# A retention and two feed-forward stages on one core: the order of the opening, and how weight conversions mix with the other vector work

## The chip, the cores and the metric

The kernel runs on one core of a Trainium2 chip. The metric is device time in microseconds (us), taken as the median of several runs of the whole kernel; a separate, profiled execution gives the trace. The engines are TensorE (PE in the rows; its weight loads are PEld), VectorE (DVE), ScalarE (ACT), GpSimd (POOL) and SyncE (SP), whose work here is to issue DMAs.

## What is computed

There are 2 sequences of 768 positions with 8 heads of 64. The retention works block by block with a state per head; `lam` is a decay rate per head:

```python
intra = einsum('bhic,bhjc->bhij', qb, kb) * Dmask       # lam ** (i - j), i >= j
out   = einsum('bhij,bhjd->bhid', intra, vb) + einsum('bhid,bhde->bhie', qb * lam_pow, kv_state)
kv_state = lam_block * kv_state + einsum('bhsd,bhse->bhde', kb * rev_pow, vb)
```

Its output, as 1536 tokens of 512, goes through two feed-forward stages: `relu(x @ w_in) ** 2 @ w_out` with 2048 inner columns, and `(sigmoid(x @ w_gate) * (x @ w_val)) @ w_out` with 1536. All inputs and the output are 32-bit floats.

## The kernel before, in words

Every matmul of the feed-forward stages is done in three passes (high part of the weights by high part of the data, low by high, high by low), so each operand is split: ScalarE copies the high part (`whi`, `gh`, `xh`), VectorE subtracts it from the source to get the low part (`wlo`, `gl`, `xl`).

**Weights.** A weight arrives as a raw tile of 512 KB (`raw`, `load_w`) and is converted to a "unit" of 256 KB. `conv_act` does the ScalarE half of it (`j`, L156, and `r`, L157), `conv_dve` the VectorE half: three operations that feed each other, shift (L179), and-or (L182) and add (L174, which writes `u`). A converted unit is also stored to DRAM for later use (L176). There are 68 units, taken in order: 32 of the first stage (two for each of its 16 steps) and 36 of the second.

**Opening (0 to 44.76 us).** The retention runs over 12 chunks of 128 positions, 0 to 5 of one sequence and 6 to 11 of the other, in pairs (0, 6), (1, 7), ... A chunk c needs its queries and keys (`q c`, 512 KB, `load_qk`; from chunk 6 on those of c + 1 as well, because the second sequence is laid out half a tile off) and its keys and values by position (`v c`, 512 KB, `load_kv`). `powers` computes the powers `W` of the decay rates and stores them to DRAM behind a row of zeros and ones; `decay_table` reads them back with a shifted address for each partition, which gives the decay masks, with the elements of one head 32 bytes apart. `att_scores` multiplies queries by keys (L297) into two PSUM banks, `att_prep` multiplies the scores by the mask on VectorE (`at`, L331), the keys by their decay on GpSimd (`kd`, L318) and the queries by theirs on GpSimd (`qd`, L306). `att_uv` makes the state's update (L364), `att_out` the output (L381, and from the second pair on L392 with the state), `att_state` adds the update to the state (L411), `att_decay` scales the state for the next pair, `att_x` splits the output. Four pairs are done in the opening, in the loop over `LEAD`; TensorE is kept going in front of it by dummy matmuls (`warm_up`, L268). The strings `FIRST`, `SIDE`, `NEXT` and `LOOP` give the order of the loads, `CONVS` the conversions that ScalarE starts at the end of each pair.

**First stage, 16 steps (`step_1`).** It computes the first 512 tokens. Step f does, on TensorE, `stage_a(f)`, twelve matmuls with the unit (f, 0), and `stage_b(f - 1)`, twelve matmuls with the unit (f - 1, 1). Beside them it splits the two units of step f + 1 (`split_w`: two copies on ScalarE at L439, two subtractions on VectorE at L441), converts two further units, applies relu and square (L484, L485) and splits the result (`split_g`: L494 on ScalarE, L496 on VectorE). Scores and outputs of the two pairs left over (4, 10) and (5, 11) are put between, by `SLOTS`. In the last steps the operands of the following stage are prepared as well (L538, L541, L552, L585 to L600).

**The rest.** From L619 on come a Strassen-like form of the remaining 1024 tokens, its output stage (L769), and the same for the second feed-forward stage.

Instructions are issued in the order in which the program writes them (`tc.manual_schedule`), so each engine goes through its own list in that order and waits at the head of it. Small pieces of work are put off by a clock that counts the matmuls written so far (`at`, `passed`, `flush`). The tiles `up` (27 buffers of 256 KB) hold units, parts, `j`, `r`, `kd`, `qd` and the like; the tiles `wp` (27 of 512 KB) hold raw weights, chunks and masks.

Of the kernel before, what the change touches and what calls it, by code (L numbers as in the profile page):

```python
# [12 lines left out]
P = 128  # L13
# [3 lines left out]
FILL = (64, 40)  # L17
# [8 lines left out]
FIRST = "q0 w v0 w"  # L26
SIDE = "q6 q7"
NEXT = "v6 q1 q8 v1 v7 q2 q9 w v2 v8 q3 q10 w v3 v9 w"
LOOP = ("", "q4 v4 w", "q11 v10 w", "w")

CONVS = (0, 1, 1, 1)
# [8 lines left out]
def retention_moe_kernel(  # L40
# [43 lines left out]
    def unit(name, dt=F32):  # L84
        return up.tile([P, 512], dt, tag="u", name=name)
# [109 lines left out]
    def run(ops):  # L195
        weave(ops, [])
# [84 lines left out]
    def pv(t):  # L281
        return t.rearrange("a (p b) -> a p b", p=4)
# [27 lines left out]
    def att_prep(c, table=None):  # L310
# [4 lines left out]
        kn = kv_t[c][:, 0, :]  # L315
        if n < SEQ_CH - 1:
            kd = kd_t[c] = unit("kd")
            nc.gpsimd.tensor_tensor(  # L318
                out=kd.rearrange("s (h d) -> s h d", h=H),
                in0=kn.rearrange("s (h d) -> s h d", h=H),  # L320
                in1=W.to_broadcast([P, H, 64]), op=ALU.mult,
            )
# [5 lines left out]
        elif 0 < n:  # L328
# [3 lines left out]
                out=dst[g], in0=pv(sc[g]), in1=(D if table is None else table)[:, g ^ s], op=ALU.mult  # L332
# [473 lines left out]
    def attend(half):  # L806
        what, k = SLOTS.get(half, (None, 0))
        if what == "scores":
            att_scores(k)
            passed(SCORES)  # L810
            if k < NCH - 1:
                load("q5 v5" if k == 10 else "q12 v11")
            return lambda: run(att_prep(k))
# [12 lines left out]
    def step_1(f):  # L826
# [3 lines left out]
        run(split_w(1, f + 1) if f + 1 < NF1 else [])  # L830
        run(conv_dve() if n > 0 else [])
# [7 lines left out]
        run(ops)  # L839
        run(conv_dve() if n > 1 else [])  # L840
# [31 lines left out]
    with tc.manual_schedule():  # L872
        powers()
        load(FIRST)
        table = decay_table()
        warm_up(WARM)
# [3 lines left out]
        load(SIDE, nc.scalar)  # L880
# [7 lines left out]
        warm_up(FILL[1])  # L888
        for c in PAIRS[0]:
            run(att_prep(c, table))  # L890
        for r in range(2):
            nc.scalar.copy(D[:, r], table[:, r])
        query(SEQ_CH + 1, qk_t[SEQ_CH + 1][:, 0, :])
        for k in range(LEAD):
# [10 lines left out]
            if k + 2 < LEAD:  # L905
                for c in PAIRS[k + 2]:
                    att_scores(c)
            load(LOOP[k])
            ops = conv_dve()
            if k + 1 < LEAD:  # L910
                nxt = PAIRS[k + 1]
                more = [op for c in nxt for op in att_prep(c)]
                run(more[:2])
# [4 lines left out]
                run(more[2:])  # L918
                weave(ops, [f for c in pair for f in att_x(c)])
            else:  # L920
# [4 lines left out]
                run(late + [f for c in pair for f in att_x(c)] + ops)  # L925
                run(att_prep(PAIRS[LEAD][0]))
# [105 lines left out]
```

## Time and profile before

| what | value |
|---|---|
| median of 3 runs | 602.79 us (602.64 to 603.23) |
| the profiled execution | 604.16 us, of which its span is 602.4 us |
| TensorE busy | 583.9 us (97%) |
| VectorE busy | 441.3 us (73%) |
| ScalarE busy | 340.1 us (56%) |
| GpSimd busy | 28.7 us (5%) |
| DMA | 126.94 MB, mean 211 GB/s |

The span is the time from the first to the last instruction of the profiled execution. TensorE's busy time counts the dummy matmuls of the opening too. A share over the whole span is a mean over stages with different limits, so the sections below look at single stretches.

### The profile page before, as it was taken

How to read it: one execution, taken by the hardware profiler on the slowest of the kernel's cores; microseconds unless marked ns; L12 is line 12 of the kernel's file. 1: busy time of each engine (PE TensorE's matmuls, PEld its weight loads, DVE VectorE, ACT ScalarE, POOL GpSimd, SP SyncE). 2: the span in 40 equal slices, each digit the busy share in tenths (PEclk: the TensorE clock that was granted, in tenths of full speed). 3: DMA queues.
4: the chain of work that ended last, by engine and by line, in shares of the span. 5: the costliest groups of instructions: out<-in, count | busy, mean ns of one | idle time of the engine just before them, and what ended most of it. 6: DMA issues, size and time to landing. Idle time of an engine off the chain costs nothing.

```text
span 602.4 us, 8777 instructions
## 1 busy us (share of the span) xinstructions
PE 583.9 (97%) x3212; PEld 481.2 (80%) x3212; DVE 441.3 (73%) x677; ACT 340.1 (56%) x558; POOL 28.7 (5%) x30
## 2 busy tenths in 40 slices
PE   7999999987999999999999999999999999999997
PEld 6887788765878888888888888888888888888885
DVE  3569999899788868888877787784777776568201
ACT  3367778988675557766557665554454455436101
POOL 2561110000000000000000000000000000000000
PEclk9799999999999999999999999999999999999999
DMA  7997696894046357999978955420433422649003
GB/s 245 412 408 261 229 314 213 272 307 139 6 169 187 128 202 243 405 410 413 406 301 278 316 186 192 129 83 19 139 123 106 139 71 73 225 168 372 1 1 139
DMA packets 52156, 126.94 MB, mean 211 GB/s; under 512 B 5777, under 2 KB 6033, under 8 KB 52114
## 3 DMA queue, kind: packets, MB, share of 16 engines
q1 hardware_dynamic: 51024, 124.41, 58.3%
q10 hardware_dynamic: 1090, 1.97, 1.0%
q8 instruction: 25, 0.41, 0.3%
q14 instruction: 17, 0.14, 0.1%
HBM read 90.71 MB, written 35.66 MB: 210 GB/s over the span
## 4 chain that ended last, share of the span: by engine, by line
PE 75%; DVE 5%; ACT 2%; issue 1%; ACTq 0%; DVEq 0%
PE p L619 32%; PE p L769 25%; PE p L453 11%; PE p L467 6%; DVE m L182 1%; DVE u L174 1%; DVE gl L496 1%; DVE xcl L541 1%; DVE wlo L441 1%; DVE m L179 0%; DVE t L552 0%; ACT r L157 0%; ACT g L485 0%; ACT gh L494 0%; ACT whi L439 0%
## 5 line engine op out<-in xcount | busy, mean ns | idle before, releaser
L619 PE MATMUL p<-xch,ah 128*128 128x512 f32 x280 | 109.5, 391 | 0.0
L619 PE MATMUL p<-xcl,ah 128*128 128x512 f32 x280 | 109.0, 389 | 0.0
L619 PE MATMUL p<-xch,al 128*128 128x512 f32 x280 | 109.0, 389 | 0.0
L769 PE MATMUL p<-g2h,whi 128*128 128x512 f32 x224 | 87.1, 389 | 0.0
L769 PE MATMUL p<-g2l,whi 128*128 128x512 f32 x224 | 87.1, 389 | 0.0
L769 PE MATMUL p<-g2h,wlo 128*128 128x512 f32 x224 | 87.1, 389 | 0.0
L619 PEld LDWEIGHTS p<-xch,ah 128*128 128x128 f32 x280 | 52.5, 188 | 12.7 <-ACT s L628 1.5
L619 PEld LDWEIGHTS p<-xch,al 128*128 128x128 f32 x280 | 52.6, 188 | 11.0
L633 DVE TENSOR_TENSOR c<-p,s 128x512 f32<-128x512 f32 x60 | 41.2, 689 | 27.5 <-PE p L619 21.6
L619 PEld LDWEIGHTS p<-xcl,ah 128*128 128x128 f32 x280 | 52.6, 188 | 10.6
L628 ACT COPY s<-p 128x512 f32<-128x512 f32 x60 | 35.2, 587 | 37.8 <-PE p L619 37.6
L156 ACT ACTIVATE j<-raw 128x512 f32<-128x512 f32 x68 | 45.7, 671 | 11.4 <-issue 5.8
L453 PE MATMUL p<-xh,wlo 128*128 128x512 f32 x160 | 44.1, 398 | 6.6 <-DVE wlo L441 6.6
L441 DVE TENSOR_TENSOR wlo<-u,whi 128x512 fp32r<-128x512 f32 x68 | 45.0, 697 | 6.9 <-ACT whi L439 4.7
L182 DVE SCALAR_TENSOR_TENSOR m<-j,m 128x512 int32<-128x512 int32 x68 | 48.4, 712 | 2.3
L174 DVE CUSTOM_DVE_ANT_0 u<-m,r 128x1024 uint16<-128x1024 uint16 x68 | 47.4, 697 | 3.7
L439 ACT CAST whi<-u 128x512 fp32r<-128x512 f32 x68 | 39.5, 618 | 18.3 <-DVE u L174 16.4
L157 ACT ACTIVATE r<-raw 128x512 int32<-128x512 uint32 x68 | 45.2, 664 | 7.8 <-PE p L769 4.5
L769 PEld LDWEIGHTS p<-g2h,whi 128*128 128x128 f32 x224 | 42.0, 188 | 8.8
L769 PEld LDWEIGHTS p<-g2l,whi 128*128 128x128 f32 x224 | 42.0, 188 | 8.7
L769 PEld LDWEIGHTS p<-g2h,wlo 128*128 128x128 f32 x224 | 42.0, 188 | 8.7
L453 PE MATMUL p<-xl,whi 128*128 128x512 f32 x160 | 43.7, 395 | 0.0
(98 smaller groups left out, 901.8 us busy)
## 6 DMA issues: line engine op xcount, KB each, us to landing
raw<-in_w SPq DMA_DIRECT2D x68, 512.0 KB, 6.3
w<-u SPq DMA_DIRECT2D x68, 256.0 KB, 3.8
u<-w SPq DMA_DIRECT2D x64, 256.0 KB, 5.1
g<-g SPq DMA_DIRECT2D x56, 256.0 KB, 4.4
g<-g SPq DMA_DIRECT2D x28, 512.0 KB, 7.6
a<-w SPq DMA_DIRECT2D x20, 512.0 KB, 4.1
kv<-in_kv SPq DMA_DIRECT2D x12, 512.0 KB, 9.9
qk<-in_qk SPq DMA_DIRECT2D x10, 512.0 KB, 8.5
```

What stands on the lines that cost most here:

```text
L156: nc.scalar.activation(j, t[:, :, 1].bitcast(F32), AF.Copy, scale=2.0**-112)
L157: nc.scalar.activation(r, t[:, :, 0].bitcast(mybir.dt.uint32), AF.Copy, scale=2.0**-29)
L174: nc.vector.tensor_tensor(out=w.bitcast(I32), in0=m, in1=r, op=ALU.add)
L182: lambda: nc.vector.scalar_tensor_tensor(out=m, in0=j, scalar=-(2**31), in1=m, op0=ALU.bitwise_and, op1=ALU.bitwise_or),
L439: nc.scalar.copy(hi, src)
L441: lambda lo=lo, src=src, hi=hi: nc.vector.tensor_tensor(out=lo, in0=src, in1=hi, op=ALU.subtract)
L453: nc.tensor.matmul(acc, lhsT=a[:, kk * P : (kk + 1) * P], rhs=b[:, kk, :], start=i == 0, stop=i == 11,)
L467: nc.tensor.matmul(acc[e], lhsT=a[:, e * P : (e + 1) * P], rhs=b, start=first and i == 0, stop=last and i == 2,)
L619: nc.tensor.matmul(acc, lhsT=w[:, col, kk * P : (kk + 1) * P], rhs=x[:, kk, :], start=start and i == 0, stop=stop and i == 5, skip_group_c ...
L628: nc.scalar.copy(s, acc)
L633: nc.vector.tensor_tensor(out=c, in0=acc, in1=s, op=ALU.add)
L769: nc.tensor.matmul(acc[e, t], lhsT=a[:, e * P : (e + 1) * P], rhs=b[:, t, :], start=first and i == 0, stop=last and i == 2,)
```

## The change

It is confined to the opening and to the order of VectorE's work in the 16 steps.

- Loads: `v0` no longer stands in `FIRST` but at the head of `NEXT`, behind the table; `q6 q7` (`SIDE`) are issued by ScalarE right behind its store of the powers, and no longer behind the decay rows and the first conversion. `NEXT` and `LOOP` are reordered; one raw weight more is loaded by the end of the opening (9 and not 8).
- Dummy matmuls: 24 and 80 in place of 64 and 40.
- The mask is copied into `D` first (one half by ScalarE, the other by VectorE), and the first pair's `at` reads that copy; before, it read the loaded table and both halves were copied afterwards by ScalarE.
- `att_keys` is split off from `att_prep` and both chunks' keys come ahead of their queries on GpSimd.
- Scores: pair k + 1 in iteration k (before: pair k + 2 in iteration k), and all four `at` of the next pair stand behind the state's update (before: two ahead of it and two behind).
- `CONVS` is (1, 1, 1, 1) in place of (0, 1, 1, 1): one unit more is converted before step 0.
- In a step, the three operations of a conversion alternate with the two low parts of the weights, and those of the second conversion with the low part of `g`; before, the low parts came first in one run and the conversion after them.

```diff
--- before.py
+++ after.py
@@ -14,7 +14,7 @@
 CH = 128
 TB = 512
 WARM = 44
-FILL = (64, 40)
+FILL = (24, 80)
 
 
 
@@ -23,12 +23,12 @@
 SLOTS = {3: ("scores", 10), 6: ("out", 4), 10: ("scores", 5), 12: ("scores", 11), 15: ("out", 5)}
 
 
-FIRST = "q0 w v0 w"
+FIRST = "q0 w w"
 SIDE = "q6 q7"
-NEXT = "v6 q1 q8 v1 v7 q2 q9 w v2 v8 q3 q10 w v3 v9 w"
-LOOP = ("", "q4 v4 w", "q11 v10 w", "w")
-
-CONVS = (0, 1, 1, 1)
+NEXT = "v0 v6 q1 q8 v1 v7 w q2 q9 w v2 v8 q3 q10"
+LOOP = ("", "w v3 v9 w", "q4 v4 w q11 v10", "w w")
+
+CONVS = (1, 1, 1, 1)
 PACE = (2, 2, 2, 2, 2, 2, 2, 2, 2, 2, 2, 2, 2, 2, 1, 0)
 
 MM = 0.2267
@@ -307,19 +307,20 @@
             out=pv(qd)[b], in0=pv(src)[b], in1=L[i // (SEQ_CH + 1)][b], op=ALU.mult
         )
 
-    def att_prep(c, table=None):
+    def att_keys(c):
+        if c % SEQ_CH < SEQ_CH - 1:
+            kd = kd_t[c] = unit("kd")
+            nc.gpsimd.tensor_tensor(
+                out=kd.rearrange("s (h d) -> s h d", h=H),
+                in0=kv_t[c][:, 0, :].rearrange("s (h d) -> s h d", h=H),
+                in1=W.to_broadcast([P, H, 64]), op=ALU.mult,
+            )
+
+    def att_prep(c):
         s, n = divmod(c, SEQ_CH)
         sc = sc_t.pop(c)
         at_t[c] = double("at")
         dst = [pv(at_t[c][:, g, :]) for g in range(2)]
-        kn = kv_t[c][:, 0, :]
-        if n < SEQ_CH - 1:
-            kd = kd_t[c] = unit("kd")
-            nc.gpsimd.tensor_tensor(
-                out=kd.rearrange("s (h d) -> s h d", h=H),
-                in0=kn.rearrange("s (h d) -> s h d", h=H),
-                in1=W.to_broadcast([P, H, 64]), op=ALU.mult,
-            )
         qt = qk_t.pop(c)[:, 0, :]
         if c == NCH - 1:
             query(NCH, qk_t.pop(NCH)[:, 0, :])
@@ -329,7 +330,7 @@
             query(c, qt)
         return [
             lambda g=g: nc.vector.tensor_tensor(
-                out=dst[g], in0=pv(sc[g]), in1=(D if table is None else table)[:, g ^ s], op=ALU.mult
+                out=dst[g], in0=pv(sc[g]), in1=D[:, g ^ s], op=ALU.mult
             )
             for g in range(2)
         ]
@@ -810,7 +811,7 @@
             passed(SCORES)
             if k < NCH - 1:
                 load("q5 v5" if k == 10 else "q12 v11")
-            return lambda: run(att_prep(k))
+            return lambda: (att_keys(k), run(att_prep(k)))
         if what == "out":
             pair = PAIRS[k]
             for c in pair:
@@ -827,8 +828,7 @@
 
         acc = stage_a(1, f)
         n = PACE[f] if len(to_conv) + len(ready) > 3 * NF2 else 0
-        run(split_w(1, f + 1) if f + 1 < NF1 else [])
-        run(conv_dve() if n > 0 else [])
+        weave(conv_dve() if n > 0 else [], split_w(1, f + 1) if f + 1 < NF1 else [])
         if n > 0:
             conv_act()
         attend(2 * f)()
@@ -836,8 +836,7 @@
             stage_b(*prev.pop())
         last = attend(2 * f + 1)
         gs, ops = split_g(elem(1, acc))
-        run(ops)
-        run(conv_dve() if n > 1 else [])
+        weave(conv_dve() if n > 1 else [], ops)
         for m in range(1, n):
             if m > 1:
                 run(conv_dve())
@@ -873,11 +872,11 @@
         powers()
         load(FIRST)
         table = decay_table()
+        load(SIDE, nc.scalar)
         warm_up(WARM)
         decay_rows()
         new_xr()
         conv_act(False)
-        load(SIDE, nc.scalar)
         load(NEXT)
         run(conv_dve())
         conv_act(False)
@@ -886,10 +885,12 @@
         warm_up(FILL[0])
         att_scores(6)
         warm_up(FILL[1])
+        nc.scalar.copy(D[:, 0], table[:, 0])
+        nc.vector.tensor_copy(D[:, 1], table[:, 1])
         for c in PAIRS[0]:
-            run(att_prep(c, table))
-        for r in range(2):
-            nc.scalar.copy(D[:, r], table[:, r])
+            att_keys(c)
+        ops = [op for c in PAIRS[0] for op in att_prep(c)]
+        run([ops[1], ops[0], ops[2], ops[3]])
         query(SEQ_CH + 1, qk_t[SEQ_CH + 1][:, 0, :])
         for k in range(LEAD):
             pair = PAIRS[k]
@@ -902,20 +903,21 @@
                 att_scores(PAIRS[1][1])
             for c in pair:
                 kv_t.pop(c)
-            if k + 2 < LEAD:
-                for c in PAIRS[k + 2]:
+            if 0 < k < LEAD - 1:
+                for c in PAIRS[k + 1]:
                     att_scores(c)
             load(LOOP[k])
             ops = conv_dve()
             if k + 1 < LEAD:
                 nxt = PAIRS[k + 1]
+                for c in nxt:
+                    att_keys(c)
                 more = [op for c in nxt for op in att_prep(c)]
-                run(more[:2])
                 for c in pair:
                     run(att_state(c))
                 for c in nxt:
                     att_decay(c, nc.scalar)
-                run(more[2:])
+                run(more)
                 weave(ops, [f for c in pair for f in att_x(c)])
             else:
                 att_scores(PAIRS[LEAD][0])
@@ -923,6 +925,7 @@
                 for c in pair:
                     run(att_state(c))
                 run(late + [f for c in pair for f in att_x(c)] + ops)
+                att_keys(PAIRS[LEAD][0])
                 run(att_prep(PAIRS[LEAD][0]))
             for m in range(CONVS[k]):
                 conv_act(False)
```

## Rows read from the trace of the kernel before

**Rows 1.** Busy time of each engine, PEclk, DMA share and GB/s in three stretches.

```profile
44.76:153.70 108.94, 100.34 (x583) 78.63 (x581) 101.36 (x160) 87.67 (x149) 7.21 (x6) 0.98 0.71 241
...
160.00:170.00 10.00, 10.00 (x45) 8.00 (x44) 9.62 (x15) 6.48 (x11) 0.00 (x0) 1.00 0.35 105
```

**Rows 2.** Timeline of TensorE: start, us, engine, line, operation, tiles, shape, count.

```profile
65.92 1.15 PE L364 MATMUL p<-kv,kd 128*64 128x64 f32 x32
...
69.79 1.19 PE L467 MATMUL p<-gh,whi 128*128 128x512 f32 x4
...
80.90 1.16 PE L297 MATMUL p<-qk 64*128 64x128 f32 x16
...
97.30 1.97 PE L381 MATMUL p<-at,kv 128*64 128x128 f32 x32
...
100.23 1.19 PE L453 MATMUL p<-xh,whi 128*128 128x512 f32 x4
...
105.81 1.07 PE L453 MATMUL p<-xh,whi 128*128 128x512 f32 x4
```

**Rows 3.** Waits from 44 to 152 us: total, times, longest.

```profile
ACT whi L439 <- DVE u L174: 16.4, 12, 2.2
...
PE p L453 <- DVE wlo L441: 6.6, 4, 2.2
```

**Rows 4.** Timeline of VectorE and ScalarE in one step.

```profile
97.39 1.46 DVE L441 TENSOR_TENSOR wlo<-u,whi 128x512 fp32r<-128x512 f32 x2
...
97.50 0.62 ACT L439 CAST whi<-u 128x512 fp32r<-128x512 f32 x1 [1.56 <-DVE u L174]
...
101.14 0.69 DVE L496 TENSOR_TENSOR gl<-g,gh 128x512 fp32r<-128x512 f32 x1 [0.50 <-ACT gh L494]
```

**Rows 5.** Groups of VectorE from 44 to 152 us: busy, mean ns, idle before.

```profile
L441 DVE TENSOR_TENSOR wlo<-u,whi 128x512 fp32r<-128x512 f32 x32 | 22.2, 709 | 1.1
...
L182 DVE SCALAR_TENSOR_TENSOR m<-j,m 128x512 int32<-128x512 int32 x29 | 21.4, 739 | 1.0
...
L174 DVE CUSTOM_DVE_ANT_0 u<-m,r 128x1024 uint16<-128x1024 uint16 x29 | 20.4, 702 | 1.4
...
L496 DVE TENSOR_TENSOR gl<-g,gh 128x512 fp32r<-128x512 f32 x15 | 10.4, 696 | 3.2 <-ACT gh L494 3.2
```

**Rows 6.** Timeline of the opening, all engines.

```profile
5.82 0.36 ACTq L234 DMA_DIRECT2D w_dram<-W  x1
...
9.49 0.33 SPq L258 DMA_DIRECT2D decay<-w_dram  x1
...
15.66 4.31 DVE L331 TENSOR_TENSOR at<-p,decay 128x512 f32<-128x512 f32 x4 [2.69 <-DMA decay<-w_dram]
...
17.79 4.10 PE L268 MATMUL p<-warm 128*128 128x128 bf16 x40
...
21.82 1.97 PE L381 MATMUL p<-at,kv 128*64 128x128 f32 x32
...
29.67 1.28 DVE L331 TENSOR_TENSOR at<-p,D 128x512 f32<-128x512 f32 x2
...
36.77 1.05 POOL L318 TENSOR_TENSOR kd<-kv,W 128x512 f32<-128x512 f32 x1
...
38.50 1.15 PE L364 MATMUL p<-kv,kd 128*64 128x64 f32 x32
...
40.95 1.75 PE L381 MATMUL p<-at,kv 128*64 128x128 f32 x28 [1.08 <-issue]
...
44.76 1.20 PE L453 MATMUL p<-xh,whi 128*128 128x512 f32 x4
```

**Rows 7.** Busy time of each engine in two stretches of the opening.

```profile
10.00:15.00 5.00, 2.58 (x47) 2.40 (x44) 2.64 (x5) 1.26 (x2) 0.00 (x0) 0.96 0.94 282
15.00:20.00 5.00, 4.22 (x37) 4.00 (x38) 4.19 (x4) 2.19 (x2) 2.28 (x2) 0.50 1.03 419
```

**Rows 8.** DMA issued at 24.5 us: KB, us from issue to landing.

```profile
kv<-in_kv SPq DMA_DIRECT2D x1, 512.0 KB, 11.2
```

## The prediction

> **What bounds the kernel now.** I read the busy times by stretch first. From 160 us on TensorE is busy 10.00 of 10.00 us [rows 1], and nearly so to the end, so a microsecond won earlier moves everything behind it forward by one: only the opening (0 to 44.76) and the 16 steps (44.76 to 153.70) can change the time. In the steps TensorE idles 108.94 - 100.34 = 8.6 us and VectorE is busy 101.36 of 108.94 [rows 1].
>
> What would the steps take without waits? The timeline of TensorE gives the work. Two groups of twelve matmuls, restart included, take 105.81 - 100.23 = 5.58 us, 2.79 each; 31 groups lie in the stretch (the sixteenth `stage_b` comes after the first Strassen block): 86.5. The retention between them takes 69.79 - 65.92 = 3.87, 100.23 - 97.30 = 2.93 and three scores of 1.16: 10.3 [rows 2]. Together 96.8, so 12.1 us of 108.94 are lost: the 8.6 of idle time, and about 2.2 to the granted clock, 0.98 in the mean [rows 1], with restarts.
>
> The waits say to whom: TensorE waits 6.6 us for `wlo`, and behind that stand twelve waits of ScalarE's `whi` on `u`, 16.4 us [rows 3]. One step shows the ring. VectorE ends a conversion and starts the low parts at 97.39; the second unit is the one just converted, so ScalarE, which waited 1.56 us for it, copies `whi` at 97.50. Its `j`, `r`, relu, square and `gh` stand behind that in its list, so `gh` is late and VectorE waits 0.50 us for it before `gl` at 101.14 [rows 4]. VectorE's idle time by groups is 1.1 (`wlo`) + 1.0 (L182) + 1.4 (L174) + 3.2 (`gl`) = 6.7 us [rows 5]. An engine with so little idle time sets the stage's length; TensorE waits for it.
>
> In the opening the timeline shows the store of the powers at 5.82, the table's load only at 9.49, the first `at` at 15.66 on the table's landing, 40 dummies from 17.79 for 4.10 us at a granted clock of 0.50, and the first output at 21.82 [rows 6, 7]. From 15 us DMA runs full at 419 GB/s; from 10 to 15 it moved 282 [rows 7].
>
> **The steps, part by part.** A step f splits units 2f + 2 and 2f + 3. Before, 2f + 3 was converted last in step f - 1; with one unit more converted in the opening it is the first of step f - 1, with `gl` and another conversion behind it. So `whi` waits for nothing fresh and the ring opens. What falls directly: `gl`'s 3.2 and `wlo`'s 1.1, 4.3 us [rows 5].
>
> The weave has its own price. An operation that reads the one before it starts 1.0 / 29 = 0.035 and 1.4 / 29 = 0.048 us after its end [rows 5], while two independent ones take 1.28 together [rows 6] where one lasts about 0.69 [rows 5], so the second starts 0.1 before the first has ended. Each such link that is parted gives about 0.12. The first conversion has both its links parted by the low parts, the second one of two by `gl`: 3 in a step, 14 converting steps, 5.0 us at most.
>
> The Trainium skill (VectorE: DVE Perf Modes, The DRAIN you can't avoid) says that the next VectorE operation does not start until the pipe is empty, chained or not. By that alone the weave would be worth nothing, and the steps would gain 4.3; the rows show a second operation starting before the first has ended, so they differ from it as far as this pair goes.
>
> Bounds for the steps: 0, if VectorE's waits come back elsewhere, and 4.3 + 5.0 = 9.3, which is below the 12.1 that are lost. I take 4.3 and a third of 5.0, 6.0 us: TensorE can only use it where it was waiting, and the preparation for the Strassen part is still packed into VectorE's list of the last steps. Against it stands one shift ahead of the first low part, at most one L182 of 0.74 [rows 5]; in a stretch where VectorE's list runs on without gaps it is paid once, not per step, and lies in the two thirds that I left out. The number of conversions within the steps stays 28.
>
> **The opening.** The store of the powers is queued behind q0, w, v0, w. Without v0 it is free of 512 KB, 1.25 us at 419 GB/s [rows 7], so the table's load would be issued at about 8.2. q6 and q7 are issued right behind that store, no longer behind the decay rows and a conversion, and so share less of the time with the table; if q7 leaves its way wholly, that is another 512 KB, 1.25. Estimate for its landing: 14.0 against 15.6, the first term whole and a quarter of the second (bounds 13.1 for both, 15.6 for neither).
>
> The Trainium skill (DMA: Bandwidth & Descriptors, Queues, rings and completion order) has each DMA engine go round between the queues packet by packet. By that the small store never stood behind v0 and the table would be no earlier: 0 in place of 1.6 for this term. The 3.7 us from store to table load [rows 6] do not decide it.
>
> What is late next: v9. It was issued at 24.5 and landed 11.2 later, at 35.7 [rows 8], the 15th load behind the table: (35.7 - 15.6) / 15 = 1.34 each, 1.25 by the rate of [rows 7]. Now it is the 17th (v0 and one w more in front): 14.0 + 17 x 1.31 = 36.3. Its keys cost 1.05 on GpSimd [rows 6], with hand-over 1.2: the last update may start at 37.5, against 38.50. From there to the first step it was 44.76 - 38.50 = 6.26, of which 1.08 was a gap before the output of chunk 9 [rows 6]. That gap goes: `at` no longer waits in two halves around the state, and TensorE has two scores and an update to do meanwhile. So the first step starts at 37.5 + 5.2 = 42.7.
>
> The other path is TensorE's own. After the scores of chunk 6 there are 80 dummies: at clock 0.50, 40 took 4.10 [rows 6], so 0.10 each, 0.05 at full clock, between 4.1 and 8.2 us. The scores in front of them wait for q7, which now passes one transfer (1.25) to three (3.75) earlier, so the dummies start between 14.0 and 16.5 in place of 17.79, and the first output comes between 18.1 and 24.7; the middle is 21.4, against 21.82. From it to the first step TensorE needs 44.76 - 21.82 - 1.08 = 21.9 us: 40.0 to 46.6, the middle 43.3. I take 42.8, between the two paths and nearer to v9's, because part of the 21.9 was waiting: a gain of 2.0. Bounds: -1.8 (the dummies at half clock throughout) and 2.9 (the table at 13.1 puts v9's path at 41.8).
>
> Copying the mask costs one strided read per engine, about 1.08 (4.31 / 4), and the four `at` fall from 4.31 to 4 x 0.64 = 2.6 [rows 6]: 3.7, a gain of 0.6 that the dummies cover. If these end early it shows, at 0.6. The extra conversion is three VectorE operations, at most 3 x 0.74 [rows 5], and two ScalarE ones of like size; the waits for v7, v8 and v9 cover both; uncovered they would cost 2.2.
>
> **Sum.** 2.0 + 6.0 = 8.0. The profiled execution has 604.16 us around a span of 602.4; it would come to 596.2. The median lies 1.37 below it: 602.79 - 8.0 = 594.8.
>
> **Rivals.**
> - *The order of VectorE's work is worth nothing* (the first rule above as a mechanism): the steps gain 4.3 less one shift of 0.4, the opening 2.0: 596.9. Against it speaks the pair at 1.28 [rows 6].
> - *The opening gives nothing*: DMA is full from 15 us [rows 7] and two more loads stand before v9; the table gains nothing (the second rule). 602.79 - 6.0 = 596.8.
> - *The last steps decide*: if TensorE's idle time lies mostly there, behind the Strassen preparation, opening the ring only moves it. Half of 4.3, and 1 to 2 of the opening: 598.8 to 600.
> - *It does not do what it says*: VectorE does the same work in the steps (28 conversions, all low parts) and was busy 93% [rows 1]; if its 6.7 idle us come back as waits for ScalarE, and v9 holds the opening, no time changes: 602 to 603.
> - *Slower*: one converted unit more is always alive in the 27 buffers. If ScalarE's `j` or `whi` then finds no free buffer until TensorE has left a group's weights, each of 14 steps waits. From 8.0 / 14 = 0.57 us a step it eats the whole gain; at the length of half a group, 1.4, the time is 602.8 + 14 x 1.4 - 8.0 = 614. For it: parts live over two groups. Against it: no wait of this sort is among the leading ones in [rows 3].
>
> **Chances.** Forecast 0.50 (own range 592.5 to 597); order worth nothing 0.13; opening nothing 0.13; last steps 0.10; no change 0.06; slower 0.08. This kernel's runs tell a change from 0.2%, 1.2 us, on. Faster: 0.50 + 0.13 + 0.13 + 0.10 = 0.86; same 0.06; slower 0.08. The range goes from 591.5 (2.9 in the opening and 8.4 of 9.3 in the steps) to 600.2, the end of the last-steps case.
>
> **What would show it.** In the new profile: almost no wait of `whi` on `u` (16.4 before); `gl` idle under 1 us; VectorE's idle time before L182 near zero, and before L174 halved; the first L453 at 42 to 43.5; the table's `at` replaced by four at about 0.68; TensorE's idle time in the steps down from 8.6 to about 3 to 4. The prediction fails if waits for buffers appear on ScalarE, if TensorE's clock drops in the longer waits of the opening and the 80 dummies run late, or if the last steps keep their 4 us of waiting for `wlo`.

## The result and the profile after

The changed kernel takes 597.09 us (median of 4 runs, 596.03 to 597.16) against 603.01 us (602.64 to 603.23) for the kernel before in the same measurement. The ratio is 0.9898, with a 95% interval of 0.9881 to 0.9915: 5.9 us are gone, where 8.0 were forecast against 602.79. The median lies inside the range and 0.1 us above the likeliest case's own range. The profiled execution took 596.03 us, its span is 594.2.

Lines of the code moved by a few numbers: L441 became L442 (`wlo`), L453 L454 and L467 L468 (the two groups of matmuls), L496 L497 (`gl`), L331 L332 (`at`), L318 L313 (`kd`), L619 L620 (the first Strassen block).

The windows of the changed kernel: the 16 steps, a stretch inside their second group, and the stretch at 160 us.

```profile
42.22:145.09 102.87, 98.88 (x583) 79.25 (x581) 98.09 (x161) 87.40 (x148) 8.43 (x7) 0.98 0.78 270
50.00:55.00 5.00, 5.00 (x17) 3.92 (x15) 4.96 (x10) 4.83 (x9) 0.00 (x0) 0.66 0.60 234
160.00:170.00 10.00, 9.98 (x44) 7.96 (x43) 8.07 (x15) 5.91 (x11) 0.00 (x0) 1.00 0.52 179
```

The steps are 6.1 us shorter than in [rows 1] (108.94 - 102.87), and TensorE idles 102.87 - 98.88 = 4.0 us of them in place of 8.6. Behind the steps it is busy 9.98 of 10.00 us, so what is won is passed on. The waits of the same stretch as in [rows 3]:

```profile
PE p L454 <- DVE wlo L442: 4.0, 3, 1.8
...
ACT j L156 <- PE p L454: 2.3, 1, 2.3
...
DVE gl L497 <- ACT gh L495: 1.7, 2, 1.1
```

The wait of `whi` on `u` (16.4 us in twelve) is gone from the list. TensorE's idle time is now three waits for `wlo` (0.38, 1.78 and 1.82 us) and nothing else. Before, it was 6.6 us for `wlo` [rows 3] and 2.0 us for ScalarE's `gh`:

```profile
PE p L467 <- ACT gh L494: 2.0, 3, 0.9
```

VectorE's groups of the changed kernel from 44 to 152 us, which answer to [rows 5]:

```profile
L442 DVE TENSOR_TENSOR wlo<-u,whi 128x512 fp32r<-128x512 f32 x31 | 21.6, 698 | 2.1 <-ACT whi L440 2.1
L182 DVE SCALAR_TENSOR_TENSOR m<-j,m 128x512 int32<-128x512 int32 x29 | 20.9, 721 | 0.0
L174 DVE CUSTOM_DVE_ANT_0 u<-m,r 128x1024 uint16<-128x1024 uint16 x29 | 20.2, 695 | 0.8
L497 DVE TENSOR_TENSOR gl<-g,gh 128x512 fp32r<-128x512 f32 x16 | 13.1, 819 | 1.8 <-ACT gh L495 1.7
```

The gaps in front of L182 and L174 fell as the weave should make them fall (1.0 to 0.0, 1.4 to 0.8). The opening, in the timelines of SyncE, VectorE, TensorE and GpSimd, answers to [rows 6]:

```profile
8.13 0.33 SPq L258 DMA_DIRECT2D decay<-w_dram  x1
...
13.59 0.62 DVE L889 COPY D<-decay 128x512 f32<-128x512 f32 x1 [0.53 <-DMA decay<-w_dram]
...
13.97 5.69 PE L268 MATMUL p<-warm 128*128 128x128 bf16 x80
...
14.32 2.48 DVE L332 TENSOR_TENSOR at<-p,D 128x512 f32<-128x512 f32 x4
...
19.59 1.97 PE L382 MATMUL p<-at,kv 128*64 128x128 f32 x32
...
37.45 0.69 PE L365 MATMUL p<-kv,kd 128*64 128x64 f32 x16 [0.31 <-POOL kd L313]
...
42.22 1.21 PE L454 MATMUL p<-xh,whi 128*128 128x512 f32 x4
...
43.81 1.20 PE L454 MATMUL p<-xh,wlo 128*128 128x512 f32 x4 [0.38 <-DVE wlo L442]
...
48.93 1.19 PE L454 MATMUL p<-xh,wlo 128*128 128x512 f32 x4 [1.78 <-DVE wlo L442]
...
49.97 1.57 PE L454 MATMUL p<-xl,whi 128*128 128x512 f32 x4
...
51.34 1.91 PE L468 MATMUL p<-gh,whi 128*128 128x512 f32 x4
...
54.29 1.07 PE L468 MATMUL p<-gl,whi 128*128 128x512 f32 x4
...
140.42 1.19 PE L454 MATMUL p<-xh,wlo 128*128 128x512 f32 x4 [1.82 <-DVE wlo L442]
```

The table is there at 13.6 (15.66 before), the last update starts at 37.45 (38.50), the first step at 42.22 (44.76). Read from this one pair of profiles, the opening gives 2.5 us and the steps 6.1, and everything looks as forecast, yet the two add to 8.6 and the medians differ by 5.9. The experiments show which of the two was not there.

### The profile page after: what moved, and what is told of

Its sections match the earlier page's. It is cut to its first block, busy times and chain, and to the rows that moved or that the text cites. A ratio compares the mean times of both kernels' runs of the same rounds, so it can differ in the third digit from the quotient of the medians.

```text
span 594.2 us, 8795 instructions
## 1 busy us (share of the span) xinstructions
PE 582.8 (98%) x3212; PEld 481.5 (81%) x3212; DVE 437.8 (74%) x678; ACT 339.1 (57%) x557; POOL 30.0 (5%) x30
## 4 chain that ended last, share of the span: by engine, by line
PE 87%; DVE 8%; issue 2%; DMA 1%; ACT 1%; ACTq 0%; POOL 0%; DVEq 0%
PE p L620 31%; PE p L770 26%; PE p L454 15%; PE p L468 10%; PE p L297 2%; PE p L382 2%; DVE xcl L542 1%; DVE m L182 1%; DVE wlo L442 1%; PE p L268 1%; DMA qk<-in_qk 1%; DVE t L553 1%; PE p L365 1%; PE p L393 1%; DVE m L179 1%
## 5 line engine op out<-in xcount | busy, mean ns | idle before, releaser
L620 PE MATMUL p<-xch,ah 128*128 128x512 f32 x280 | 109.5, 391 | 0.3 <-DVE c L634 0.2
L620 PE MATMUL p<-xch,al 128*128 128x512 f32 x280 | 109.0, 389 | 0.0
L620 PE MATMUL p<-xcl,ah 128*128 128x512 f32 x280 | 109.0, 389 | 0.0
L620 PEld LDWEIGHTS p<-xch,ah 128*128 128x128 f32 x280 | 52.5, 188 | 13.2 <-ACT s L629 1.7
L620 PEld LDWEIGHTS p<-xch,al 128*128 128x128 f32 x280 | 52.6, 188 | 11.1
L620 PEld LDWEIGHTS p<-xcl,ah 128*128 128x128 f32 x280 | 52.6, 188 | 10.6
L629 ACT COPY s<-p 128x512 f32<-128x512 f32 x60 | 35.2, 587 | 37.8 <-PE p L620 37.5
L442 DVE TENSOR_TENSOR wlo<-u,whi 128x512 fp32r<-128x512 f32 x68 | 45.5, 698 | 8.0 <-ACT whi L440 6.8
L174 DVE CUSTOM_DVE_ANT_0 u<-m,r 128x1024 uint16<-128x1024 uint16 x68 | 47.8, 702 | 3.2
L182 DVE SCALAR_TENSOR_TENSOR m<-j,m 128x512 int32<-128x512 int32 x68 | 48.4, 712 | 1.3
L454 PE MATMUL p<-xh,wlo 128*128 128x512 f32 x160 | 43.3, 392 | 4.0 <-DVE wlo L442 4.0
L454 PE MATMUL p<-xl,whi 128*128 128x512 f32 x160 | 43.4, 394 | 0.0
L454 PE MATMUL p<-xh,whi 128*128 128x512 f32 x160 | 43.2, 392 | 0.0
```

Of the source, the lines that this page charges most:

```text
L174: nc.vector.tensor_tensor(out=w.bitcast(I32), in0=m, in1=r, op=ALU.add)
L182: lambda: nc.vector.scalar_tensor_tensor(out=m, in0=j, scalar=-(2**31), in1=m, op0=ALU.bitwise_and, op1=ALU.bitwise_or),
L442: lambda lo=lo, src=src, hi=hi: nc.vector.tensor_tensor(out=lo, in0=src, in1=hi, op=ALU.subtract)
L454: nc.tensor.matmul(acc, lhsT=a[:, kk * P : (kk + 1) * P], rhs=b[:, kk, :], start=i == 0, stop=i == 11,)
L620: nc.tensor.matmul(acc, lhsT=w[:, col, kk * P : (kk + 1) * P], rhs=x[:, kk, :], start=start and i == 0, stop=stop and i == 5, skip_group_c ...
L629: nc.scalar.copy(s, acc)
```

## The experiments

Diffs are against the kernel before unless it is said otherwise; times are medians, each beside the kernel before in the same measurement.

**The whole change again.**

> The whole change again, as a base for the others. The theory (steps and opening add up) expects a ratio near 0.990 and again a first step near 42.2 us and a Strassen start near 145.1 us in its trace. The rival, that the profiled execution of before was itself a slow one because of the half-clock stretch of TensorE at 147.7 us, expects the profiled span to fall by clearly less than 8.2 us if both are profiled again, and the steps to last over 104 us here.

597.80 against 603.22 us, 0.9901 (0.9883 to 0.9919). In its profile the first step starts at 43.11, later than the 42.22 above, and Strassen at 147.12. So its steps last 104.0 us, just over what the rival said, and its span of 596.2 lies 6.2 and not 8.2 us under the one before: the first pair of profiles made the change look larger than it is. But the half-clock stretch that the rival names is no mark of the kernel before; this profile has one too (a granted clock of 0.50 from 52.5 to 55 us), and so has the changed kernel's first one (50 to 55 us, above). Counted from their second group on, the steps take the same time in both profiles of the change (table below).

**The opening alone.** The changed kernel, with the steps and the number of conversions as before:

```diff
-LOOP = ("", "w v3 v9 w", "q4 v4 w q11 v10", "w w")
-CONVS = (1, 1, 1, 1)
+LOOP = ("", "w v3 v9 w", "q4 v4 w q11 v10", "w")
+CONVS = (0, 1, 1, 1)
...
-        weave(conv_dve() if n > 0 else [], split_w(1, f + 1) if f + 1 < NF1 else [])
+        run(split_w(1, f + 1) if f + 1 < NF1 else [])
+        run(conv_dve() if n > 0 else [])
...
-        weave(conv_dve() if n > 1 else [], ops)
+        run(ops)
+        run(conv_dve() if n > 1 else [])
```

> The opening alone: all of the change but the unit converted ahead and the weave. The theory expects the first step near 42.2 us and a gain of 2.0 to 2.5 us (ratio 0.9960). The rival that VectorE's list sets the end of the steps whatever the start expects the same, since the list starts with the first step. The rival that the opening's gain is lost in the steps (a longer wait for the first low parts) expects under 1 us.

602.84 against 603.22 us, 0.9994 (0.9981 to 1.0007): no change that can be measured. VectorE's and GpSimd's timelines of this kernel around the end of the opening:

```profile
41.28 0.69 DVE L423 TENSOR_TENSOR xl<-p,xh 128x512 fp32r<-128x512 f32 x1
41.88 1.20 DVE L182 SCALAR_TENSOR_TENSOR m<-j,m 128x512 int32<-128x512 int32 x1
43.11 1.65 DVE L174 CUSTOM_DVE_ANT_0 u<-m,r 128x1024 uint16<-128x1024 uint16 x1
44.69 0.74 DVE L412 TENSOR_TENSOR S<-p,tt 128x256 f32<-128x256 f32 x2
45.35 1.28 DVE L442 TENSOR_TENSOR wlo<-u,whi 128x512 fp32r<-128x512 f32 x2
...
41.48 1.04 POOL L313 TENSOR_TENSOR kd<-kv,W 128x512 f32<-128x512 f32 x1 [0.41 <-PE p L382]
42.48 1.73 POOL L306 TENSOR_TENSOR qd<-qk,L 128x512 f32<-128x512 f32 x1
```

and the same place in the kernel before:

```profile
42.19 0.68 DVE L182 SCALAR_TENSOR_TENSOR m<-j,m 128x512 int32<-128x512 int32 x1
42.91 0.69 DVE L174 CUSTOM_DVE_ANT_0 u<-m,r 128x1024 uint16<-128x1024 uint16 x1
...
44.44 1.28 DVE L441 TENSOR_TENSOR wlo<-u,whi 128x512 fp32r<-128x512 f32 x2
```

Here the conversion of the third pair runs beside GpSimd's products and its two long operations take 1.20 and 1.65 us in place of 0.68 and 0.69. The first low parts, for which the first group waits, start at 45.35 and not at 44.44, though the first step itself started 0.5 earlier (44.24). The stretching is not peculiar to the new order: with the loads of before, five of seven profiles have such an operation at the same place (L182 takes 1.75 us in the unit ahead alone, L174 1.65 in the weave alone). So this pair shows that the start of the first step was not passed on, and leaves open why.

**The unit ahead alone.**

```diff
-LOOP = ("", "q4 v4 w", "q11 v10 w", "w")
-CONVS = (0, 1, 1, 1)
+LOOP = ("", "q4 v4 w", "q11 v10 w", "w w")
+CONVS = (1, 1, 1, 1)
```

> One unit more converted and loaded ahead alone, in the kernel before. The theory (the ring of u, whi, gh, gl opens) expects the waits of whi on u to fall from 16.4 us to under 3, gl's idle time from 3.2 to under 1, and a gain of 3 to 4.5 us (ratio 0.994). The rival that the last steps decide expects the waits to move and a gain of at most 1.5 us.

599.78 against 603.22 us, 0.9939 (0.9927 to 0.9951). Its waits and `gl`'s group:

```profile
PE p L453 <- DVE wlo L441: 6.3, 4, 2.2
...
ACT whi L439 <- DVE u L174: 3.4, 2, 2.1
```

```profile
L496 DVE TENSOR_TENSOR gl<-g,gh 128x512 fp32r<-128x512 f32 x16 | 12.1, 754 | 0.7 <-ACT gh L494 0.6
```

The ring is open: `whi` waits 3.4 us in place of 16.4, and `gl` 0.7 in place of 3.2. TensorE's wait for `wlo` hardly moved.

**The weave alone.** Both lines of `step_1` woven as in the changed kernel, nothing else.

```diff
-        run(split_w(1, f + 1) if f + 1 < NF1 else [])
-        run(conv_dve() if n > 0 else [])
+        weave(conv_dve() if n > 0 else [], split_w(1, f + 1) if f + 1 < NF1 else [])
...
-        run(ops)
-        run(conv_dve() if n > 1 else [])
+        weave(conv_dve() if n > 1 else [], ops)
```

> The weave alone, in the kernel before. The theory expects a small gain, 0 to 2 us (VectorE's idle time before L182 goes to near zero, two operations overlap), while the ring stays closed, so the wait of whi on u stays above 10 us. The rival that order within VectorE's list is worth nothing expects 0 to 0.5 us slower, since the first low part stands one shift further back.

598.26 against 603.22 us, 0.9911 (0.9899 to 0.9924): 5.0 us, where the sum had 1.7 (on top of the unit ahead) and the text above 0 to 2. Of the waits, these three lines:

```profile
ACT whi L439 <- DVE u L174: 12.8, 12, 2.1
...
PE p L453 <- DVE wlo L441: 5.3, 4, 1.8
DVE gl L496 <- ACT gh L494: 4.2, 7, 0.9
```

The ring is still closed, and `gl` waits even longer. So this gain is of another kind than that of the unit ahead. VectorE's timeline in one step shows it:

```profile
103.60 0.69 DVE L496 TENSOR_TENSOR gl<-g,gh 128x512 fp32r<-128x512 f32 x1 [0.71 <-ACT gh L494]
104.21 0.68 DVE L182 SCALAR_TENSOR_TENSOR m<-j,m 128x512 int32<-128x512 int32 x1
104.93 0.69 DVE L174 CUSTOM_DVE_ANT_0 u<-m,r 128x1024 uint16<-128x1024 uint16 x1
105.54 0.42 DVE L179 TENSOR_SCALAR m<-j 128x512 int32<-128x512 int32 x1
105.87 0.69 DVE L441 TENSOR_TENSOR wlo<-u,whi 128x512 fp32r<-128x512 f32 x1
106.47 0.69 DVE L182 SCALAR_TENSOR_TENSOR m<-j,m 128x512 int32<-128x512 int32 x1
107.07 0.69 DVE L441 TENSOR_TENSOR wlo<-u,whi 128x512 fp32r<-128x512 f32 x1
```

L174 reads what the L182 in front of it wrote, and starts 0.72 us after it (104.21, 104.93). Operations that don't read each other start 0.60 apart (105.87, 106.47, 107.07), 0.09 before the first has ended. By these starts a link that is parted is worth 0.72 - 0.60 = 0.12, the price in the prediction.

**The weave at `gl` alone.** Only the second of the two lines above.

> Only the second half of the weave, in the kernel before: the low part of g between shift and and-or of the second conversion. It parts one dependent pair per step and hides no wait for a copy of ScalarE. The theory (a parted pair saves 0.12 us of VectorE's time, 14 steps) expects 1.0 to 1.7 us. The rival (the weave wins by doing a shift while ScalarE copies whi, so only its first half counts) expects 0 to 0.3 us.

600.17 against 603.72 us, 0.9944 (0.9929 to 0.996): 3.55 us, more than twice what the parted pairs should give. The shift of the second conversion now stands in front of `gl`, and `gl`'s idle time falls from 3.2 to 1.1 with the ring as closed as before (`whi` waits 15.4). VectorE's busy time does not fall (98.99 against 98.58 in the table below), so at `gl` the saving by parted pairs does not show; what shows is the idle time that the shift fills.

**No link parted, the second conversion whole in front of `gl`.**

```diff
-        run(ops)
         run(conv_dve() if n > 1 else [])
+        run(ops)
```

> In the kernel before, the second conversion of a step as a whole ahead of the low part of g: no dependent pair is parted, nothing overlaps more than before, but VectorE has 1.8 us of work while it would wait for gh. If the second half of the weave won by filling that wait (idle time of gl 3.2 us before, 0.4 behind gh with the shift in front), this gives 2 to 3.5 us as well. If it won by parted pairs and overlap, this gives 0, or a loss of up to 1 us because gl comes later for TensorE.

599.13 against 603.78 us, 0.9921 (0.9904 to 0.9937).

```profile
L496 DVE TENSOR_TENSOR gl<-g,gh 128x512 fp32r<-128x512 f32 x16 | 11.4, 712 | 0.0
```

```profile
PE p L467 <- DVE gl L496: 3.0, 2, 2.1
```

VectorE no longer waits for `gh` at all; the cover is paid with 3.0 us of TensorE waiting for `gl`. Still 4.65 us are won, more than the 2 to 3.5 expected of filling the wait, with the same operations in another order and no link parted within a conversion. So the time alone can't tell the two ways of winning apart; the busy and idle times of the profiles do, further down.

**Unit ahead and weave, the opening as before** (the edits of "the unit ahead alone" and "the weave alone" together).

> The unit ahead and the weave together in the kernel before, with the opening of before. Alone they gave 3.4 and 5.0 us. If they take the same idle time of TensorE twice (the theory now: what TensorE can win in the steps is bounded by its own waits), the two together give 5.0 to 6.0 us, about as much as the whole change (ratio 0.991). If they add up, 8.4 us (ratio 0.986).

597.35 against 603.72 us, 0.9896 (0.9879 to 0.9914): the whole result without any of the new opening. The two gains alone were 3.4 and 5.0, together they give 6.4, between the two expectations.

**The change without the unit ahead** (the changed kernel with `LOOP` and `CONVS` as in the run of the opening alone).

> The whole change without the unit converted ahead: opening and weave. If the opening gives 0.4 us, as alone, and the weave 5.0: 5.0 to 5.5 us (ratio 0.991), with the waits of whi on u back at over 10 us in the trace and no loss by them. If the ring of u, whi and gh matters beside the weave: 2 us less than the whole change, ratio 0.994.

597.95 against 603.72 us, 0.9908 (0.9887 to 0.9929). On top of the weave, the unit ahead is not worth enough to be measured here, though `whi` waits 13.8 us for `u` again. Neither is the new opening: the weave alone gave 0.9911.

**The three waits that are left, by order.** The changed kernel, with the first step's split taken to the end of the opening, and the Strassen preparation begun earlier:

```diff
-        weave(conv_dve() if n > 0 else [], split_w(1, f + 1) if f + 1 < NF1 else [])
+        weave(conv_dve() if n > 0 else [], split_w(1, f + 1) if 0 < f < NF1 - 1 else [])
...
-                run(late + [f for c in pair for f in att_x(c)] + ops)
+                run(late + [f for c in pair for f in att_x(c)] + split_w(1, 1) + ops)
...
-        prepare_a(keys[0], T1)
+        prepare_a(keys[0], T1 - 14.0)
...
-        combine_x([T1 + d for d in (-30, -25, -15, -13, -11, -9, -7, 1, 2.5, 5.5, 7)])
+        combine_x([T1 + d for d in (-40, -36, -32, -27, -22, -17, -11, 1, 2.5, 5.5, 7)])
```

> The whole change with two edits at the places where its trace still shows TensorE waiting for wlo: the low parts of step 1 are taken ahead of the last conversion of the opening and of the scores of chunk 4 (wait of 1.78 us at the second group), and the preparation of the Strassen part is put 10 to 14 us earlier (wait of 1.82 us at the sixteenth). If VectorE's order at the two ends is what is left, the waits fall to under 0.5 us each and the time by 3 to 4 us against the whole change: 593 to 595 us, ratio 0.985. If VectorE's total work sets the length, the waits come back elsewhere and the time stays at 597.

599.54 against 603.72 us, 0.9937 (0.992 to 0.9954), slower than the change by some 2 us. TensorE's timeline:

```profile
51.35 1.21 PE L468 MATMUL p<-gl,whi 128*128 128x512 f32 x4 [1.29 <-DVE gl L497]
...
61.87 1.19 PE L454 MATMUL p<-xh,wlo 128*128 128x512 f32 x4 [1.43 <-DVE wlo L442]
...
128.09 2.07 PE L468 MATMUL p<-gl,whi 128*128 128x512 f32 x4 [1.98 <-DVE gl L497]
```

The waits of 1.78 and 1.82 at 48.93 and 140.42 became waits of 1.29, 1.43 and 1.98 elsewhere. Work that VectorE has to do either way was carried to places where TensorE waits more: from the second group to Strassen it idles 102.79 - 97.03 = 5.8 us here, 3.6 in the changed kernel.

**Taking VectorE work out of the way of the first groups.** The changed kernel; the masks' products of chunk 4 and one conversion leave the end of the opening:

```diff
+        if f == 0:
+            run(att_prep(PAIRS[LEAD][0]))
+        if f == 4:
+            run(conv_dve())
...
-            ops = conv_dve()
+            ops = conv_dve() if k + 1 < LEAD else []
...
-                run(att_prep(PAIRS[LEAD][0]))
```

> The whole change with a lighter front: the last conversion of the opening is left to the steps (one more in step 4 makes up for it), and the scores of chunk 4 are multiplied by the mask at the end of step 0 and no longer in front of it. VectorE's list gets 3 us shorter ahead of the low parts of step 1. If VectorE's total up to a given step is what counts, the wait of 1.78 us at the second group goes, with the half-clock stretch behind it, and 1.5 to 3 us are won against the whole change: 594.5 to 596 us. If the wait only moves to the next step, as it did when only the order was changed, the time stays at 597 to 598.

595.25 us (594.31 to 596.31) against 603.78, 0.9861 (0.9843 to 0.9879): faster than both kernels. In TensorE's timeline the second group has no wait any more, and the waits that are left stand elsewhere:

```profile
43.67 1.19 PE L454 MATMUL p<-xh,wlo 128*128 128x512 f32 x4 [0.68 <-DVE wlo L442]
...
60.49 1.20 PE L454 MATMUL p<-xh,wlo 128*128 128x512 f32 x4 [1.28 <-DVE wlo L442]
...
138.18 1.20 PE L454 MATMUL p<-xh,wlo 128*128 128x512 f32 x4 [1.82 <-DVE wlo L442]
```

Their sum is hardly less than in the changed kernel (3.8 us, 4.0 there). From the second group to Strassen this profile is 99.03 - 96.93 = 2.1 us shorter; 0.5 of that is idle time of TensorE and 1.6 its busy time, which is what a half-clock stretch costs (last section). This profile has no such stretch, the changed kernel's has one. The text above expected the wait and the stretch to go together; one profile can't show that the edit removes the stretch.

**The same with the conversion whole in front of `gl`**, and **that with the opening of before.** The first adds to the edit just shown:

```diff
-        weave(conv_dve() if n > 1 else [], ops)
+        run(conv_dve() if n > 1 else [])
+        run(ops)
```

The second has the same `step_1` and the same edits at the end of the opening, put into the kernel before, with its extra unit:

```diff
-LOOP = ("", "q4 v4 w", "q11 v10 w", "w")
-CONVS = (0, 1, 1, 1)
+LOOP = ("", "q4 v4 w", "q11 v10 w", "w w")
+CONVS = (1, 1, 1, 1)
```

> The version with the lighter front, and in it the second conversion of a step as a whole ahead of the low part of g. If work in front of the wait for gh is what lets VectorE run ahead, its lead at the late preparation grows and the last wait for wlo (1.82 us) shrinks: 0.5 to 1.5 us less than the 595.25 of the lighter front, ratio 0.984. If that lead is already as long as TensorE's order allows, no change from 0.9861, or a little more by waits of TensorE for gl.

> The same edits of the steps, unit ahead and lighter front, but with the opening of before: loads, dummies, mask and scores as they were. If the new opening is worth nothing, as with it alone (0.4 us) and with the steps alone (597.35 against 597.80), the time is within 1 us of the run beside it. If it is worth the 2.0 us of the forecast once the front of the steps is light, this one is 1.5 to 2.5 us slower.

597.37 against 603.73 us, 0.9894 (0.9881 to 0.9907), and 598.67, 0.9918 (0.9893 to 0.9943). In the first, the whole conversion in front of `gl` costs 2.1 us against the lighter front: TensorE waits 3.3 us for `gl`. The intervals of the two overlap, and the second's six times fall into two groups (595.82 to 597.23 and 600.11 to 600.33), so it says nothing on the opening.

## Why the prediction came out as it did

Where the time went shows best if the steps are counted from their second group (the second L453 or L454 of `xh,whi`, at 47.61 before) to the first Strassen block, because the first group still carries what the opening left. All numbers are from the timeline of TensorE and the windows of each profile; the clock is TensorE's granted clock in that stretch.

```profile
47.61 1.07 PE L453 MATMUL p<-xh,whi 128*128 128x512 f32 x4
```

| kernel | second group at | from there to Strassen | TensorE busy | VectorE busy | VectorE idle | clock |
|---|---|---|---|---|---|---|
| before | 47.61 | 106.09 | 97.49 | 98.58 | 7.51 | 0.98 |
| opening alone | 48.32 | 106.27 | 97.51 | 98.68 | 7.59 | 0.98 |
| unit ahead alone | 46.20 | 102.59 | 96.04 | 99.34 | 3.25 | 0.98 |
| weave alone | 46.09 | 101.19 | 95.86 | 94.79 | 6.40 | 0.98 |
| weave at `gl` alone | 46.70 | 103.73 | 97.03 | 98.99 | 4.74 | 0.98 |
| conversion whole in front of `gl` | 47.02 | 101.04 | 94.83 | 96.58 | 4.46 | 1.00 |
| unit ahead and weave | 46.83 | 98.58 | 94.21 | 94.00 | 4.58 | 1.00 |
| after | 46.06 | 99.03 | 95.43 | 94.32 | 4.71 | 0.98 |
| the whole change again | 48.12 | 99.00 | 95.40 | 93.14 | 5.86 | 0.98 |
| VectorE work taken out | 45.91 | 96.93 | 93.83 | 94.09 | 2.84 | 1.00 |

Each row at 0.98 holds one stretch of some 5 us partly at the lower level of the clock, the rows at 1.00 none. In the changed kernel it cost 1.6 us (last section), so TensorE's busy time and the length compare directly only between rows with the same clock. Between the two profiles of the change VectorE's busy time differs by 1.2 us.

For the opening, the means over seven profiles with the loads of before and seven with the new ones. They are of different kernels, some with edits at the end of the opening, so they are rough.

| when, us | loads of before | new loads |
|---|---|---|
| VectorE first reads the table | 15.84 | 13.94 |
| first output | 18.26 | 18.20 |
| last update | 37.98 | 37.63 |
| first step | 43.54 | 42.65 |
| VectorE's first low parts | 43.69 | 43.71 |
| second group | 46.74 | 46.80 |

The first output in the unit ahead alone, with the loads of before (21.82 in [rows 6]):

```profile
16.41 0.41 PE L381 MATMUL p<-at,kv 128*64 128x128 f32 x2
```

- **What bounds it: right.** Only the opening and the steps changed, and 6.6 of TensorE's 8.6 us of waiting in the steps were for VectorE's `wlo`; the other 2.0, for ScalarE's `gh`, went with the change. What was left out: the rest of the kernel gives 0.4 us back (span less the start of Strassen: 602.4 - 153.70 = 448.7 before, 594.2 - 145.09 = 449.1 after).
- **The ring, 4.3 us: right in mechanism, near in size.** The unit ahead alone cut VectorE's idle time by 7.51 - 3.25 = 4.3 us, the stretch by 3.5 and the time by 3.4.
- **The weave, a third of 5.0: mis-sized.** It cut VectorE's busy time by 98.58 - 94.79 = 3.8 us alone and by 99.34 - 94.00 = 5.3 on top of the unit ahead, where 42 links at 0.12 give 5.0. Most of it shows at the low parts of the weights: from the weave at `gl` alone to both it is 98.99 - 94.79 = 4.2. At `gl` it does not show, and the whole conversion in front of `gl` takes 2.0 us off the busy time without parting a link, so the price per link is borne out as a size and not link by link. The choice of a third, argued from TensorE being able to use it only where it waited, was too little: alone the 3.8 us came with 106.09 - 101.19 = 4.9 us less stretch, and on top of the unit ahead the weave was worth 6.4 - 3.4 = 3.0 us of time in place of 1.7.
- **Adding the two: wrong in the other direction.** The ring and the second weave fill the same idle time before `gl`: the weave at `gl` alone cuts VectorE's idle time by 2.8 with the ring closed. So opening the ring was not the only cure for the late `gh`; a piece of work in front of the waiting operation does as well. Alone the two gave 3.4 + 5.0 = 8.4 us, together 6.4. That the sum had 6.0 for them is luck: too little for the weave and nothing taken off for the overlap nearly cancel.
- **The rule by which the order is worth nothing: not borne out.** That rival put the weave at zero; alone it is worth 5.0 us, and operations that don't read each other start 0.60 us apart, 0.72 where one reads the other. The Trainium skill (VectorE: DVE Perf Modes, The DRAIN you can't avoid) has the next operation start only when the pipe is empty, and adds that one which is not held starts earlier. The trace agrees with the addition as far as these pairs go.
- **The opening, 2.0 us: this step failed.** The new times came nearly as forecast: the table's load at 8.13 (8.2), the table at 13.6 (14.0), the last update at 37.45 (37.5), the first step at 42.22 (42.8 was taken). But the gain was taken against the 44.76 of one execution. Six other profiles with the loads of before start the first step at 42.61 to 43.88, 43.34 in the mean. The forecast also took off the 1.37 us by which that execution lay above the median; the late start, 44.76 - 43.34 = 1.4, is of that size, so it may have been counted twice. And what the opening does win is spent on the way. The table's 1.9 us are gone at the first output: the 21.82 of [rows 6] was late too, and with the loads of before five of seven profiles have it at 16.41 to 17.34. With the new loads it comes at 17.72 to 19.59, behind the 80 dummies; no run took fewer of these. The 0.9 us that are left at the first step are gone at VectorE's first low parts, which start no sooner. With the new loads the first group waits 0.38 to 1.55 us for them, and in all seven profiles it is longer until the second group than in any with the loads of before (3.83 to 5.01 us, 2.85 to 3.59); why VectorE is no sooner there stays open. That the opening wins nothing that can be measured is shown three times: alone, with the weave (0.9908 against 0.9911), and with weave and unit ahead (0.9898 and 0.9901 against 0.9896).
- **The rivals' numbers.** With 0 for the opening the sum is 602.79 - 6.0 = 596.8, the rival that the opening gives nothing; the rival that the order is worth nothing stands at 596.9. Both lie within 0.3 us of 597.09, so the time does not choose between them; the runs do, in favour of the first, though its reason (two more loads in front of v9, a table no earlier) was not the cause. By its own terms the last-steps rival comes to 598.6 to 599.6, not 598.8 to 600, on which the upper end of the range rests.
- **The round between the queues: not borne out.** With v0 out of the way the table's load is issued at 8.13 to 8.62 in seven profiles, with it at 9.46 to 10.07 in seven others; the store in front of it is issued at 5.81 to 5.95 in all of them. No run moved v0 alone. By the Trainium skill (DMA: Bandwidth & Descriptors, Queues, rings and completion order) each DMA engine takes turns between the queues packet by packet. The prediction drew from it that v0 would not matter, and the 1.3 us between the two sets of profiles speak against that.
- **Signs that were named.** Right: `whi` on `u`, the gaps before L182 and L174, the start of the first step, TensorE's idle time (4.0, forecast 3 to 4); the wait for `wlo` in the last steps fell from 1.78 + 2.20 to 1.82. Wrong: `gl`'s idle time is 1.8 and not under 1. In the unit ahead alone it is 0.7 and in the weave alone 4.2, so it is the weave that brings VectorE to `gl` before ScalarE has `gh`. One sign of failure did appear, small: with the unit ahead `j` waits for TensorE, whose results it does not read (2.3 + 1.2 + 0.6 us in the changed kernel, never from 44 to 152 us before), as the slower rival said of buffers. TensorE's own waits are all for `wlo`, so it did not set the time.

What is still open: why the first step's start differs by more than 2 us between kernels with the same loads (42.61 to 44.76 with those of before, 41.53 to 44.24 with the new ones), and by 0.9 us between the two profiles of the changed kernel. In two profiles the scores of chunk 6 began late (15.78 before, 16.05 in the weave at `gl` alone, 12.86 to 13.43 in the other five) after 3.2 and 3.5 us of waiting for their load, q6 or q7. These two have the late first outputs as well, but one of them starts the first step at 43.77, before one of the five others (43.88); no run varied that load alone.

## What to carry to other kernels

Take the baseline of a stretch whose start hangs on loads from several executions, not from one profile, and don't correct for the same excess twice. In the engine that is busy over nine tenths of a stretch, shorter chains counted here nearly in full, but each idle gap counts once, however many edits would fill it. Moving its work inside the stretch moved the waits and cost 2 us; taking work away from in front of the first groups brought 0.9861 in place of 0.9898. Before such a last gain is put down to the waits, look at the granted clock: in the profile 1.6 of 2.1 us were the clock's.

## What was not expected of the hardware

- **VectorE beside GpSimd.** Operations with both inputs in SBUF were stretched while GpSimd multiplied (L182 1.20 and L174 1.65 us against 0.68 and 0.69, in the opening alone), while `xl`, which reads PSUM, kept 0.69 beside the same product. The Trainium skill (SBUF — State Buffer, Who interferes with whom) says that VectorE's instructions with two SBUF inputs contend with GpSimd's that read SBUF, and that those with at most one, outside the modes that take both ports, do not. The trace agrees.
- **The clock after a wait.** In the changed kernel the granted clock was 0.66 from 50 to 55 us, that is, partly at the lower of its two levels (1.2 and 2.4 GHz), after TensorE had waited 1.78 us; from the start of `xl` by `whi` to that of `gl` by `whi` it took 54.29 - 49.97 = 4.3 us. In the kernel with unit ahead and weave alone TensorE waited 1.78 us in front of the same matmuls and the clock stayed at 1.00; its timeline has the same stretch in 53.46 - 50.73 = 2.7 us:

```profile
50.73 1.08 PE L453 MATMUL p<-xl,whi 128*128 128x512 f32 x4
...
53.46 1.07 PE L467 MATMUL p<-gl,whi 128*128 128x512 f32 x4
```

So the length of that wait does not decide it by itself, and 1.6 us hang on it. What does decide it is not shown.
